# Identity products of other widths, the first chunk's gates loaded first, and another order in front of the first block

## The chip, the cores and the metric

The kernel runs on one core of a Trainium2 chip. The metric is device time in microseconds of one execution. A smaller time is better. Engines are called by the profile's names: PE (TensorE matmul), PEld (its weight loads), DVE (VectorE), ACT (ScalarE), POOL (GpSimd), SP (SyncE, whose queue issues nearly all DMAs).

## What is computed

A gated linear attention with 4 batches of 8 heads, 768 tokens and head size 40, followed by a two-layer network over the 3072 tokens with softplus between its layers:

```python
for t in range(S):
    m_new = np.maximum(f_gate[:, :, t] + m, i_gate[:, :, t])
    f_stab = np.exp(f_gate[:, :, t] + m - m_new)
    i_stab = np.exp(i_gate[:, :, t] - m_new)
    C = f_stab * C + i_stab * np.einsum('bhd,bhe->bhde', vt, kt)
    n = f_stab * n + i_stab * kt
    y[:, :, t] = sigmoid(o_gate[:, :, t]) * np.einsum('bhde,bhe->bhd', C, qt) / np.maximum(np.abs(nq), 1.0)
x = y.transpose(0, 2, 1, 3).reshape(B * S, H * D)      # 3072 x 320
h = x @ w_in                                           # 320 x 2048
g = np.maximum(h, 0.0) + np.log1p(np.exp(-np.abs(h)))
out = g @ w_out                                        # 2048 x 320
```

The weights arrive as 64-bit floats and are taken apart on the chip.

## The kernel before

The recurrence is done in chunks of 128 tokens (six per batch). A step is one chunk of one batch; 24 steps in the order of `ORDER`, which begins with the first chunk of each batch (steps 0 to 3 are named 1_0, 2_0, 0_0 and 3_0 in tile names). Three steps make a token tile of 384 rows, and 16 blocks of the hidden layer are computed for each of the eight tiles. A block is eight products into one PSUM bank `hp` (`X` against the high and low parts of `w_in`, `wih` and `wil`, L1154 for the first 32 blocks and L1006 later), softplus on ACT (L908, L910), the low part on DVE (`gl`, L916), and nine products into three banks `po` (L988, later L1006). The first block needs the whole of `X0`, that is, all of steps 0 to 2.

In front of the first block stand, in this order of need:

- **The gates.** `first_gates` (L167) loads the gates of the first chunk (`g0`, L172), scans them on DVE, takes the exponent on ACT, and spreads the result over partitions with small products by an identity matrix: `spread` (L163, into bank `po1`, copied out as `gT`) and, in `decays`, L429 (into `hp`, scanned by DVE at L445 as `pw`). `later_gates` (L216) does the same for the other chunks in two parts, tiles `gt0` and `gt1`, whose input gates are spread by `spread_inputs` (L206, copied to `gT` at L214). L156 spreads the decays of `gt0` into the pair of banks `pa`.
- **Steps 0 to 2.** Each has scores (L499), states (L516), a copy `cp`, values (L615 and L623) into a pair of banks (`pa` or `po2`), their sum on DVE (`y1z` L462, `yy` L644), a gate on POOL (`x`, L669), three transposes on PE (L752) and two halves of `X` on ACT and DVE.
- **The weights** of the first blocks, taken apart by `single` (L277 on), each part on the engine that `PICK` names (V DVE, G POOL, A ACT).
- **Identity products.** `keep_warm` (L771) multiplies the identity matrix by itself, `k` units of 128 columns, up to `cols` units in one product, into `po1`; nobody reads the result. Such a product of 32-bit floats shows as two records in the trace. Where it stands is called `k0`, `k1` and so on in `WHEN`; its `k` stands in `WARM`, its `cols` in `COLS`.

The program is recorded in the order of the numbers in `WHEN`, from low to high (a negative number is before the first block, a positive one counts products from there), and `in_order` (L114) makes each engine run its instructions in the recorded order. So the table decides what stands behind what on each engine, on SP's queue too. DMAs are all issued by SP but three. Behind the first blocks the same table runs the other steps among the products.

Of the kernel before, what the change touches and what calls it, by code (L numbers as in the profile page):

```python
# [18 lines left out]
L = 128  # L19
# [12 lines left out]
NCHAIN = B * H  # L32
# [12 lines left out]
def mlstm_moe_kernel(  # L45
# [121 lines left out]
    def first_gates():  # L167

        nc.vector.memset(fg0, 0.0)
        fg, ig = g0[:NCHAIN, 0], g0[:NCHAIN, 1]  # L170
        m = p1.tile([NCHAIN, L + 1], F32, tag="y1", name="m0")
        nc.sync.dma_start(g0[:NCHAIN], gates[:, :, 0:L].rearrange("g p s -> p g s"))  # L172
# [598 lines left out]
    def keep_warm(k, cols):  # L771
        assert not begun
        for i in range(0, k, cols):
            n = min(cols, k - i)
            nc.tensor.matmul(wm[:, 0:n], ident, ident.unsqueeze(1).broadcast_to([128, n, L]), start=True, stop=True)  # L775
# [431 lines left out]
    def finished(t):  # L1207
        return all(s in ended for s in range(t * NG, (t + 1) * NG))

    WHEN = {'l0': -292.75, 'p0': -281.3125, 'p1': -293.5, 'l1': -277.507812, 'p2': -277.578125, 'wl0': -278,  # L1210
# [186 lines left out]
```

## Time and profile before

| | us |
|---|---|
| three runs | 426.43, 429.14, 429.2 (median 429.14) |
| the profiled execution, whole time | 427.4 |
| its span, first to last instruction | 425.6 |
| PE busy | 418.3 (98%) |
| DVE busy | 272.8 (64%) |
| ACT busy | 210.8 (50%) |
| POOL busy | 62.8 (15%) |

The profiled execution lies inside the range of the three runs; 1.8 us of its time lie around the span. PE's share of busy time counts the identity products too, and the page's chain that ended last is PE for 93% of the span.

### The profile page before, as it was taken

The numbers are of one execution on the slowest core, as the hardware profiler recorded it, in microseconds if no ns is written. First come the engines' busy times: TensorE is split into PE (matmuls) and PEld (weight loads), VectorE is DVE, ScalarE is ACT, GpSimd is POOL, SyncE is SP. The second block draws the span as 40 slices with busy tenths as digits, with TensorE's granted clock in tenths as the row PEclk, the third lists the DMA queues.
The fourth block names the chain that finished last, engine by engine and source line by source line (L and its number), as shares of the span: only waits on it lengthen the run. The fifth ranks groups of instructions, "written<-read, shape, count | busy, mean of one in ns | idle before, by whom it ended". The sixth has DMA issues, their size and how long they took to land.

```text
span 425.6 us, 16026 instructions
## 1 busy us (share of the span) xinstructions
PE 418.3 (98%) x6866; PEld 403.9 (95%) x6866; DVE 272.8 (64%) x544; ACT 210.8 (50%) x443; POOL 62.8 (15%) x104
## 2 busy tenths in 40 slices
PE   8899999999999999999999999999999999999996
PEld 7789989999999999999999999999999999999996
DVE  6788899496867776749566675758567664522221
ACT  5588996776536243634336443534335433333332
POOL 2544634244454000000000000000000000000000
PEclk9999999999999999999999999999999999999999
DMA  6895975755275746173364536284264330001001
GB/s 192 269 294 165 271 217 156 223 176 162 64 193 160 189 118 185 49 204 93 76 171 116 127 115 163 64 159 138 67 186 104 74 114 24 2 2 48 2 3 48
DMA packets 51240, 55.17 MB, mean 130 GB/s; under 512 B 5568, under 2 KB 41312, under 8 KB 51168
## 3 DMA queue, kind: packets, MB, share of 16 engines
q1 hardware_dynamic: 50736, 53.65, 45.9%
q8 instruction: 54, 0.88, 0.8%
q10 hardware_dynamic: 432, 0.49, 0.4%
q14 instruction: 18, 0.15, 0.2%
HBM read 45.97 MB, written 8.14 MB: 127 GB/s over the span
## 4 chain that ended last, share of the span: by engine, by line
PE 93%; ACT 2%; DMA 1%; issue 1%; SPq 1%; DVE 1%; POOL 1%; ACTq 0%; POOLq 0%
PE hp L1006 31%; PE po L1006 29%; PE po L988 9%; PE hp L1154 8%; PE po L775 3%; PE hp L499 3%; PE pa L683 2%; PE pa L695 2%; DMA flast<-fl_d 1%; PE hp L516 1%; PE hp L429 1%; PE pa L499 1%; PE pa L516 0%; PE po L163 0%; PE pa L623 0%
## 5 line engine op out<-in xcount | busy, mean ns | idle before, releaser
L1006 PE MATMUL hp<-X,wih 64*128 64x384 f32 x1056 | 177.6, 337 | 0.0
L908 ACT ACTIVATE gh<-hp 128x384 fp32r<-128x384 f32 x80 | 39.3, 491 | 176.3 <-PE hp L1006 150.6
L1006 PEld LDWEIGHTS hp<-X,wih 64*128 64x128 f32 x1056 | 123.8, 185 | 1.8 <-POOLq L1017 0.3
L1006 PE MATMUL po<-woh,g 64*128 64x320 f32 x564 | 123.4, 306 | 0.1
L916 DVE TENSOR_TENSOR gl<-full,gh 128x384 fp32r<-128x384 f32 x48 | 26.8, 558 | 94.3 <-ACT full L910 93.8
L1006 PE MATMUL hp<-X,wil 64*128 64x384 f32 x384 | 81.2, 333 | 0.0
L1006 PEld LDWEIGHTS po<-woh,g 64*128 64x128 f32 x564 | 78.5, 185 | 0.0
L1006 PE MATMUL po<-woh,gh 64*128 64x320 f32 x294 | 68.0, 310 | 0.0
L1006 PE MATMUL po<-wol,gh 64*128 64x320 f32 x294 | 66.7, 306 | 0.0
L1006 PE MATMUL po<-woh,gl 64*128 64x320 f32 x294 | 66.4, 305 | 0.0
L1006 PE MATMUL po<-wol,g 64*128 64x320 f32 x282 | 63.9, 306 | 0.0
L1006 PEld LDWEIGHTS hp<-X,wil 64*128 64x128 f32 x384 | 58.0, 185 | 0.0
L910 ACT ACTIVATE full<-hp 128x384 f32<-128x384 f32 x96 | 46.7, 487 | 0.0
L1154 PE MATMUL hp<-X,wih 128*128 128x384 f32 x192 | 45.1, 341 | 0.3 <-DVE gl L916 0.3
L1006 PEld LDWEIGHTS po<-woh,gh 64*128 64x128 f32 x294 | 42.3, 184 | 0.0
L1006 PEld LDWEIGHTS po<-woh,gl 64*128 64x128 f32 x294 | 41.3, 185 | 0.0
L1006 PEld LDWEIGHTS po<-wol,gh 64*128 64x128 f32 x294 | 41.2, 185 | 0.0
L1006 PEld LDWEIGHTS po<-wol,g 64*128 64x128 f32 x282 | 39.2, 184 | 0.3 <-issue 0.3
L1154 PEld LDWEIGHTS hp<-X,wih 128*128 128x128 f32 x192 | 33.1, 188 | 1.0 <-DVE gl L916 0.6
L916 DVE TENSOR_TENSOR g<-full,g 128x384 fp32r<-128x384 f32 x48 | 26.7, 557 | 10.6 <-PE po L1006 7.2
L445 DVE TENSOR_TENSOR_SCAN pw<-fb,ident 128x512 f32<-128x512 f32 x21 | 26.6, 1268 | 0.0
L908 ACT ACTIVATE g<-hp 128x384 fp32r<-128x384 f32 x48 | 23.7, 493 | 0.1
(185 smaller groups left out, 700.0 us busy)
## 6 DMA issues: line engine op xcount, KB each, us to landing
vt<-in_vk SPq DMA_DIRECT2D x24, 324.0 KB
qk<-in_qk SPq DMA_DIRECT2D x48, 160.0 KB
fb<-fz_d SPq DMA_DIRECT2D x42, 128.0 KB
wo<-in_w_out SPq DMA_DIRECT2D x8, 640.0 KB
wr<-in_w_in SPq DMA_DIRECT2D x8, 512.0 KB
eg<-in_oT SPq DMA_DIRECT2D x6, 576.0 KB
yd<-y SPq DMA_DIRECT2D x36, 96.0 KB
out<-ob SPq DMA_DIRECT2D x21, 160.0 KB
```

The lines of the kernel that those rows point to most:

```text
L429: nc.tensor.matmul(z.fb[y * Q : (y + 1) * Q, j, :], ident[:, k : k + 1].broadcast_to([128, Q]), fg0, start=True, stop=True,)
L445: nc.vector.tensor_tensor_scan(z.pw.rearrange(flat), z.fb.rearrange(flat), ident4.rearrange(flat), 0.0, ALU.mult, ALU.add)
L499: nc.tensor.matmul(z.ga[x][y * Q : (y + 1) * Q, (i * NQ + q) * Q : (i * NQ + q + 1) * Q], z.k[rows, g, ts], z.q[rows, g, ts], start=True, ...
L683: nc.tensor.matmul(gc[out, x, c0 : c0 + Q], (z.cm if q else z.old)[rows, g * E : g * E + w], z.q[rows, g, q * Q : (q + 1) * Q], start=True ...
L695: nc.tensor.matmul(gc[i * PP : i * PP + w, y, c0 : c0 + Q], z.via[rows, e0 : e0 + w], z.pm[rows, j, q * Q : (q + 1) * Q], start=True, stop ...
L775: nc.tensor.matmul(wm[:, 0:n], ident, ident.unsqueeze(1).broadcast_to([128, n, L]), start=True, stop=True)
L908: nc.scalar.activation(gh, hp, AF.Softplus)
L910: nc.scalar.activation(full, hp, AF.Softplus)
L916: nc.vector.tensor_tensor(gl, full, gh, op=ALU.subtract)
L988: nc.tensor.matmul(po[j], a[:, j * 128 : (j + 1) * 128], w[:, f, :], start=(first and left[j] == 2), stop=(last and left[j] == 0),)
L1006: nc.tensor.matmul(out, *a, **k)
L1154: nc.tensor.matmul(hp, a, r, start=(i == 0), stop=(i == len(seq) - 1))
```

## The change

Three edits of code. The DMA of `g0` is issued ahead of the memsets that it waited for, so the zeroing of `g0` leaves out the partitions that it writes and becomes two memsets. `keep_warm` can put small products (32 rows out, 16 columns, line 775 of the kernel after) ahead of its units, as many as a new table `SMALL` says. And the tables change: nearly all numbers of `WHEN`, `COLS` (up to three units in one product), `WARM`, and some of `PICK`. All lines behind L172 move down by one to eight.

```diff
     def first_gates():
 
-        nc.vector.memset(fg0, 0.0)
+        nc.sync.dma_start(g0[:NCHAIN], gates[:, :, 0:L].rearrange("g p s -> p g s"))
+        nc.vector.memset(fg0[NCHAIN:64], 0.0)
+        nc.vector.memset(fg0[64:128], 0.0)
         fg, ig = g0[:NCHAIN, 0], g0[:NCHAIN, 1]
         m = p1.tile([NCHAIN, L + 1], F32, tag="y1", name="m0")
-        nc.sync.dma_start(g0[:NCHAIN], gates[:, :, 0:L].rearrange("g p s -> p g s"))
...
-    def keep_warm(k, cols):
+    def keep_warm(k, cols, small):
         assert not begun
+        for _ in range(small):
+            nc.tensor.matmul(wm[0:32, 0, 0:16], ident[:, 0:32], ident[:, 0:16], start=True, stop=True)
...
-    COLS = {0: 2, 2: 2, 3: 1, 4: 1, 6: 1, 7: 1, 9: 1, 10: 1, 11: 1, 12: 1, 17: 2, 20: 1}
-    WARM = {0: 15, 1: 2, 2: 1, 3: 3, 4: 2, 5: 3, 6: 3, 7: 4, 8: 0, 9: 2, 10: 3, 11: 4, 12: 2, 13: 0, 14: 2, 15: 4,
-        16: 1, 17: 2, 18: 1, 19: 0, 20: 4, 21: 0}
+    SMALL = {8: 0, 17: 0, 2: 0, 0: 0, 14: 0, 3: 0, 9: 0, 19: 0, 13: 4, 4: 0, 7: 0, 18: 0, 15: 0, 1: 0, 6: 2, 5: 0,
+        10: 0, 20: 0, 16: 1, 21: 0, 11: 0, 12: 0}
+    COLS = {0: 2, 2: 1, 3: 1, 4: 3, 6: 1, 7: 3, 9: 2, 10: 2, 11: 1, 12: 1, 17: 1, 20: 1, 5: 1, 15: 3, 18: 2, 14: 2,
+        19: 3, 21: 1, 8: 3, 1: 3, 13: 3, 16: 3}
+    WARM = {0: 15, 1: 1, 2: 4, 3: 4, 4: 1, 5: 4, 6: 0, 7: 0, 8: 0, 9: 1, 10: 5, 11: 2, 12: 4, 13: 0, 14: 2, 15: 7,
+        16: 0, 17: 0, 18: 4, 19: 0, 20: 0, 21: 0}
...
-            once(f"k{k}", us(at), keep_warm, WARM.get(k, n), COLS.get(k, 2))
+            once(f"k{k}", us(at), keep_warm, WARM.get(k, n), COLS.get(k, 2), SMALL.get(k, 0))
```

On PE, between the scores of the second step (into `po2`) and the states that follow, stood before (`hp`, `pa`, `po` are PSUM banks, `gt` the later gates, `ident` the identity matrix):

```order
L775 MATMUL po_80<-ident 128x128 x3
L775 MATMUL po_80<-ident 128x256
L615 MATMUL pa<-cp_0_263,qk_0_191 64x41 x8
L623 MATMUL pa<-vi_0_261,pw_0_232 64x41 x16
L163 MATMUL po_80<-ident,gt_128 64x16 x8
L775 MATMUL po_80<-ident 128x256 x2
L775 MATMUL po_80<-ident 128x128 x2
```

At the same place on PE stands now:

```order
L778 MATMUL po_80<-ident 128x128 x4
L163 MATMUL po_80<-ident,gt_160 64x16 x8
L616 MATMUL pa<-cp_0_285,qk_0_191 64x41 x8
L624 MATMUL pa<-vi_0_303,pw_0_223 64x41 x16
L778 MATMUL po_80<-ident 128x128 x5
```

The spread of `gt0` has gone from behind the values of the first step (L615, L623) to ahead of them, so that it no longer stands right in front of identity products, which write the bank that ACT copies `gT` from.

On PE, at the first two blocks and a half, stood before (the third transposes of `X0` first; `hp_72`, `hp_73`, `hp_74` are the banks of blocks 0, 1 and 2):

```order
L775 MATMUL po_80<-ident 128x128 x4
L752 MATMUL hp_74<-ident,x_0_589 128x128 x3
L775 MATMUL po_80<-ident 128x128 x4
L1154 MATMUL hp_72<-X_564,wih 128x384 x2
L775 MATMUL po_80<-ident 128x128 x3
L1154 MATMUL hp_72<-X_564,wih 128x384 x2
L1154 MATMUL hp_72<-X_564,wil 128x384 x2
L1154 MATMUL hp_72<-X_564,wih 128x384 x2
L1154 MATMUL hp_73<-X_564,wih 128x384 x2
L156 MATMUL pa<-ident,d_342 128x32 x2
L1154 MATMUL hp_73<-X_564,wih 128x384 x2
L615 MATMUL pa<-cp_0_654,qk_0_434 64x41 x8
```

At the same place on PE stands now:

```order
L775 MATMUL po_80<-ident 32x16 x6
L778 MATMUL po_80<-ident 128x128 x2
L753 MATMUL hp_74<-ident,x_0_614 128x128 x3
L778 MATMUL po_80<-ident 128x256 x2
L778 MATMUL po_80<-ident 128x128
L775 MATMUL po_80<-ident 32x16
L1157 MATMUL hp_72<-X_584,wih 128x384 x4
L1157 MATMUL hp_72<-X_584,wil 128x384 x2
L1157 MATMUL hp_72<-X_584,wih 128x384 x2
L1157 MATMUL hp_73<-X_584,wih 128x384 x4
L616 MATMUL pa<-cp_0_649,qk_0_434 64x41 x8
L624 MATMUL pa<-values_in,pw_0_512 64x41 x16
```

The three units inside the first block are gone, and L156 has left block 1: it comes five products behind the values of the fourth step (L624), in front of the second product of block 2, and both write `pa`.

On SP's queue the program began with these DMAs (`g` the first chunk's gates, `gt` the later ones, `wr` the first weights):

```order
L223 DMA gt_128<-in_gates 32x2x256
L172 DMA g_103<-in_gates 32x2x128
L223 DMA gt_142<-in_gates 32x2x384
L317 DMA wr_152<-in_w_in 128x2x512
L320 DMA wr_152<-in_w_in 64x256 x2
```

It begins with these now:

```order
L169 DMA g_103<-in_gates 32x2x128
L224 DMA gt_136<-in_gates 32x2x384
L224 DMA gt_160<-in_gates 32x2x256
L318 DMA wr_166<-in_w_in 128x2x512
L321 DMA wr_166<-in_w_in 64x256 x2
```

The first chunk's gates have moved up one place, and the 256 columns of `gt0` went from first to third.

## Rows read from the trace of the kernel before

**Rows 1.** The page, part 1: busy time, share of the span, instructions.

```profile
PE 418.3 (98%) x6866; PEld 403.9 (95%) x6866; DVE 272.8 (64%) x544; ACT 210.8 (50%) x443; POOL 62.8 (15%) x104
```

**Rows 2.** Busy time by stretch: engines' us (instructions), granted clock, DMA share, GB/s.

```profile
16.48:32.87 16.39, 16.04 (x369) 14.39 (x369) 12.99 (x29) 13.76 (x23) 7.19 (x10) 1.00 0.87 271
32.87:100.00 67.13, 66.57 (x844) 62.18 (x843) 55.17 (x104) 53.48 (x113) 30.58 (x43) 1.00 0.70 201
100.00:422.00 322.00, 321.88 (x5435) 315.79 (x5433) 192.40 (x384) 135.68 (x296) 17.72 (x28) 1.00 0.39 102
```

**Rows 3.** The chain that ended last, first 70 us: start, us, what (x records).

```profile
1.71 5.31 PE po L775 x16
...
10.21 0.85 PE po L775 x4
...
13.17 1.30 PE po L775 x8
...
15.41 1.07 issue
...
16.81 0.59 PE po L163 x16
...
17.42 0.22 ACT gT L214
...
17.69 1.57 PE po L775 x8
...
21.73 1.28 PE po L775 x6
...
23.63 1.09 PE po L775 x8
...
25.32 1.31 PE po L775 x10
...
30.45 1.09 PE po L775 x8
```

**Rows 4.** Timeline of PE: start, us, line, tiles, shape, records, idle before.

```profile
17.69 1.57 PE L775 MATMUL po<-ident 128*128 128x256 f32 x8 [0.31 <-ACT gT L214]
...
31.97 1.06 PE L775 MATMUL po<-ident 128*128 128x128 f32 x8
32.87 0.60 PE L1154 MATMUL hp<-X,wih 128*128 128x384 f32 x2
33.31 0.83 PE L775 MATMUL po<-ident 128*128 128x128 f32 x6
34.02 0.62 PE L1154 MATMUL hp<-X,wih 128*128 128x384 f32 x2
...
34.82 0.86 PE L1154 MATMUL hp<-X,wih 128*128 128x384 f32 x4
35.60 0.63 PE L156 MATMUL pa<-ident,d 32*128 32x32 f32 x4
```

**Rows 5.** Timeline of DVE, same columns.

```profile
3.21 0.47 DVE L178 TENSOR_TENSOR_SCAN m<-g,m 32x128 f32<-32x128 f32 x1 [2.05 <-DMA g<-in_gates]
...
8.43 1.22 DVE L445 TENSOR_TENSOR_SCAN pw<-hp,ident 128x512 f32<-128x512 f32 x1 [0.29 <-PE hp L429]
...
32.17 0.56 DVE L796 CAST X<-hp 128x384 fp32r<-128x384 f32 x1 [0.21 <-PE hp L752]
...
37.96 0.50 DVE L462 TENSOR_TENSOR y1z<-pa,fcT 64x328 f32<-64x328 f32 x1 [1.14 <-PE pa L623]
38.50 0.50 DVE L644 TENSOR_TENSOR yy<-pa,y1z 128x328 f32<-128x328 f32 x1
```

**Rows 6.** Timeline of SP's queue: the issue of the first chunk's gates.

```profile
1.19 0.41 SPq L172 DMA_DIRECT2D g<-in_gates  x1
```

**Rows 7.** DMA queues from 13 to 17 us: packets, MB, share of 16 engines.

```profile
q1 hardware_dynamic: 556, 1.26, 96.4%
q8 instruction: 1, 0.02, 2.1%
```

More of the change, by code (lines that the diff above doesn't have):

```diff
@@ L1208, in finished @@
         return all(s in ended for s in range(t * NG, (t + 1) * NG))
-    WHEN = {'l0': -292.75, 'p0': -281.3125, 'p1': -293.5, 'l1': -277.507812, 'p2': -277.578125, 'wl0': -278,
[65 rows of a table removed]
-    COLS = {0: 2, 2: 2, 3: 1, 4: 1, 6: 1, 7: 1, 9: 1, 10: 1, 11: 1, 12: 1, 17: 2, 20: 1}
-    WARM = {0: 15, 1: 2, 2: 1, 3: 3, 4: 2, 5: 3, 6: 3, 7: 4, 8: 0, 9: 2, 10: 3, 11: 4, 12: 2, 13: 0, 14: 2, 15: 4,
-        16: 1, 17: 2, 18: 1, 19: 0, 20: 4, 21: 0}
+    WHEN = {'l0': -278.414062, 'p0': -302.25, 'p1': -300.25, 'l1': -303.25, 'p2': -279.449219, 'wl0': -278,
[66 rows of a table added]
+    SMALL = {8: 0, 17: 0, 2: 0, 0: 0, 14: 0, 3: 0, 9: 0, 19: 0, 13: 4, 4: 0, 7: 0, 18: 0, 15: 0, 1: 0, 6: 2, 5: 0,
[4 more added lines that the diff above has]
+        16: 0, 17: 0, 18: 4, 19: 0, 20: 0, 21: 0}
     PICK = {'wl2': 'V', 'oh6': 'G', 'wl3': 'V', 'mgi7': 'V', 'ol1': 'V', 'ol3': 'V', 'wh5': 'A', 'wi61': 'V',
         'ol2': 'V', 'mgo5': 'V', 'wi50': 'V', 'ol5': 'V', 'gb0': 'V', 'wi01': 'A', 'wl1': 'V', 'xh2': 'V',
[1 row of a table removed]
[1 row of a table added]
         'mgi5': 'A', 'wi51': 'G', 'wm50': 'G', 'wh6': 'V', 'wl6': 'V', 'cq8': 'V', 'gc1': 'V', 'vi2': 'V',
[2 rows of a table removed]
[2 rows of a table added]
         'wl4': 'V', 'x5': 'V', 'vi6': 'A', 'cq6': 'V', 'mgi6': 'V', 'old7': 'A', 'cp7': 'V', 'cq7': 'V', 'wi60': 'G',
```

148 rows, old and new, of tables (PICK, WHEN) are left out of this document.

## The prediction

> **What bounds the kernel now.** The page's busy times come first [rows 1]: PE is busy for 98% of the span and the next engine, DVE, for 64%. A mean over stages doesn't say what a change in one stage is worth, so the second view is busy time by stretch [rows 2]. From 32.87 us, where the first block's first product starts [rows 4], to 100 us PE is busy for 66.57 of 67.13 us, and from 100 to 422 us for 321.88 of 322.00. From the first block on the time is PE's own work, and an order that frees another engine there has 0.6 us to win at most. The third view, the chain that ended last [rows 3], shows what a busy PE in front of the block is worth: a good part of it is L775, the identity products, whose result nobody reads. So the time can move in two ways: by the moment at which the first block begins, and by PE time behind it that is no product of a block.
>
> **Identity products.** Each is two records. Counted in units of 128 columns there were 15 at the start (5.31 us), then groups of 3, 5, 6, 5, 4, 5, 4, 4 and 4, and 3 more inside the first block, 58 in all. The order has 54 now: the same 15, then 4, 4, 5, 2, 7, 5, 1, 4, 2 and 5, none in the block, and seven small ones. The chain has most of the old groups [rows 3]: 0.85, 1.30, 1.57, 1.28, 1.09, 1.31 and 1.09 us, sum 8.49. The group at 31.97 us lasts until 32.87, 0.90, with transposes and wide products as neighbours, and a group of four that has transposes ahead of it is put at the same; the one in the block lasts from 33.31 to 34.02, 0.71 [rows 4]. Together 11.00 us behind the first 15.
>
> The new groups are priced from these. Four single units take 1.09 and five take 1.31 [rows 3]: 0.22 a unit, and 1.09 - 0.88 = 0.21 for coming from smaller products and going back. About half of that, 0.1, is left where one neighbour is 128 wide, as the 0.90 shows. A double takes (1.28 - 0.21 - 0.22) / 2 = 0.43. No triple is in the trace: between three halves of a double, 0.65, and three singles, 0.66; I take 0.65. No small one is either: the nearest row is the eight spreads of L163, 0.59 us, 0.07 each, and the lower bound is nothing; I take 0.07, as their shape is nearly the same. Then the groups are 4: 1.09; 4: 1.09; 5: 1.31; a double: 0.64; two triples and a single: 1.30 + 0.22 + 0.21 = 1.73; two doubles and a single: 1.28; a single: 0.32; 4 beside transposes: 0.98; six small and two singles: 0.42 + 0.44 + 0.10 = 0.96; two doubles, a single and a small one: 0.86 + 0.22 + 0.12 = 1.20. Sum 10.60, of which all stands in front of the block. **Term: 10.60 - 11.00 = -0.40**, made of +0.31 in front and -0.71 in the block; between -0.9 (small ones free) and 0.
>
> **The first chunk's gates first: 0.** The first scan waited 2.05 us for this DMA, which was issued at 1.19 us behind `gt0` [rows 5, 6]; without that DMA's issue, of its own length, ahead of it, it can land about 0.4 us sooner. But what the gates feed on PE, the spreads at L163 and L429, stand behind the 15 identity units, which still end at 1.71 + 5.31 = 7.02 us, and DVE's first `pw` scan at 8.43 waits for those spreads, not for gates [rows 5]. The cover is PE's own filling; without it the gain would be 0.4. The later `gt0` lands behind one DMA more, and its scan stands behind the first chunk's in any case. One decoding step of the first weights has moved from ACT to DVE, ahead of that `pw` scan. It isn't in the trace in this form; below it costs nothing (0.29 us of idle time in front of the scan), above as much as the scan itself, 1.22 us [rows 5], less this idle time. Behind it wait `pw`, POOL's `vw` and the first states on PE, and in front of these PE now has a group of four identity units, 1.09 us, and the spread for the third step, which has moved up; so 0.
>
> **The spread of `gt0` moved ahead.** Before, identity products at 17.69 waited 0.31 us until ACT had copied `gT` out of their bank (copy 17.42, 0.22 us) [rows 3, 4]. Now the spread stands ahead of the first step's values, which cover the copy. **Term: -0.31**; 0 if another copy is late at the next identity group (the part 1 spread has a 256-column unit and the second step's values behind it first).
>
> **The wait at 15.41.** In the middle of L623's equal products PE stood for 1.07 us, and the chain calls it "issue": nothing that the profile shows was waited for [rows 3]. In 13 to 17 us the program's DMAs took 96.4% of the DMA engines, and one packet of an instruction queue was among them [rows 7]. I read it as PE having run out of fetched instructions. If the fetch ends at a given moment, the 0.59 us of L163's spread [rows 3], which now runs before the wait and not behind it, fills that much of it: -0.59. If the fetch is set off by PE's own progress, the wait moves along and keeps its length: 0. **Term: -0.30**, half way; the bounds are -1.07 (gone) and +1.07 (once more elsewhere). [...]
>
> **L156 behind the values.** This spread writes `pa`. Before, it came ahead of the values of the fourth step. Now it comes five products behind them, and DVE has to read those values out of `pa` first: 37.96 to 39.00, 1.04 us for `y1z` and `yy` [rows 5]. Five products cover (35.60 - 34.82) / 4 = 0.20 each [rows 4] at most, so some 0.9 to 1.0, and a wait of 0.1 is left with DVE free at once. DVE had 1.14 us idle before `y1z`, but the values now come about 0.6 us sooner in PE's order, since L156 (0.63 us at 35.60) has left its place ahead of them. **Term: +0.25**, between 0 and 0.8. Behind L156 in PE's queue wait the rest of block 2 and all blocks.
>
> The other moves in the tables (weights on other engines, later steps, DMAs of `wr2` ahead of `fz_d`) lie beside the full PE of [rows 2] and are put at 0, within the 0.56 us that PE stood idle from 32.87 to 100.
>
> **Sum: -0.40 - 0.31 - 0.30 + 0.25 = -0.76.** The first block's first product comes 0.3 us sooner (about 32.6), and what follows gains 0.71 and loses 0.25. On the profiled execution's 427.4 us that gives 426.6. The median of the three runs is 429.14, which would give 428.4; the four executions known lie from 426.43 to 429.2, so a median of the changed kernel can fall anywhere between, and I put it at 427.3.
>
> **The rivals.**
> - *Nothing moves* (chance 0.25). The identity products were filling in waits, and what is taken out comes back as idle time in front of X0: the last cast of X0 ended at 32.73 [rows 5], 0.14 us ahead of the first block. For it speaks that short distance; against it that groups of 4 to 6 units stood ahead of work whose inputs were long there, and that the 0.71 in the block had ready products on both sides. It gives 427.4 by the profiled execution, 428.1 by the same reckoning as above.
> - *Slower: L156 takes the place of the waits removed* (0.12). If DVE reaches `y1z` more than a microsecond late, PE stands before block 2 for that long. It decides once the wait is over 0.25 + 0.76 = 1.0 us. DVE has weights and `gl` of block 0 ahead of it, each 0.5 to 1.2 us. With 2 us the sum is +1.0: 428.4 by the profiled execution, 429.1 as above.
> - *The clock falls* (0.05). [...] Less filling can mean more idle time. The price is in the start: the first 15 units took 5.31 us, and seven doubles and a single at later prices are 3.3, so one stay at the low level cost 2.0 us. It gives 428.6 to 429.3. [...]
> - *Both waits go* (0.08): the 1.07 at 15.41 vanishes and the small products cost nothing: -0.9 - 0.31 - 1.07 + 0.1 = -2.2, 425.2 by the profiled execution, 425.9 as above.
>
> **How the numbers follow.** The forecast has 0.50. The terms' bounds add up to -2.3 and +1.9 on 427.4, 425.1 to 429.3; with the spread of the runs at both ends I take 424.8 to 429.8. One per cent, 4.3 us, is about what a measurement of this kernel can tell from no change, and no case reaches it. What is left for it is the spread of the runs, 2.8 us, on top of the outer cases: faster 0.05, same 0.91, slower 0.04.
>
> **What would show it.** In the profile after: the first block's first product near 32.6; PE standing less than 1.07 us inside the first step's values and not at all before the identity units that follow; no identity product after the first block begins; a wait of 0 to 0.8 us before L156; PE full from 100 us on. Wrong would be a first block at 33 us or later, a wait of over 1 us before block 2's second product, a granted clock under 1.00, or PE idle for over 1 us between 33 and 100 us.

## The result, and the profile after

The changed kernel takes 429.97 us against 428.23 us, medians of 22 runs each; the ratio is 1.0054, 95% interval 1.0036 to 1.0071 (the quotient of these medians is 1.0041). Three of the changed kernel's runs (435 to 438 us, granted clock 0.98) and the profiled run of block_new below (434.44 us, 0.98) were in a slower state, and the ratios leave such runs out. The change is about half a per cent slower, and the forecast was 0.2% faster. The profiled execution takes 428.87 us, 1.47 more than that of before, with a span of 427.1 us.

The page of the kernel after, part 1, answers to [rows 1]:

```profile
PE 419.0 (98%) x6866; PEld 404.3 (95%) x6866; DVE 274.2 (64%) x549; ACT 211.4 (49%) x444; POOL 62.3 (15%) x99
```

The page says nothing of the loss: PE is busy for the same 98%. Busy time by stretch does [rows 2], here of the kernel after:

```profile
16.48:32.87 16.39, 15.75 (x355) 13.25 (x350) 13.42 (x30) 12.91 (x21) 7.77 (x10) 1.00 0.95 281
32.87:100.00 67.13, 65.09 (x834) 60.75 (x833) 55.55 (x106) 53.30 (x115) 29.37 (x39) 1.00 0.66 195
100.00:422.00 322.00, 321.72 (x5433) 316.14 (x5432) 192.66 (x384) 137.06 (x296) 17.98 (x28) 1.00 0.40 104
```

PE's idle time from 32.87 to 100 us has gone from 0.56 to 2.04 us. So the loss lies behind the start of the first block, where the prediction had written 0. Two rows of PE hold most of it (timeline of PE after: start, us, line, tiles, shape, records, idle before and what ended it); the three rows above them are from the front:

```profile
21.09 0.44 PE L624 MATMUL po<-vi,pw 64*64 64x41 f32 x16 [0.18 <-issue]
...
31.63 0.55 PE L753 MATMUL hp<-ident,x 128*128 128x128 f32 x3 [0.46 <-POOL x L670]
...
33.36 1.32 PE L1157 MATMUL hp<-X,wih 128*128 128x384 f32 x4
...
53.27 0.44 PE L1157 MATMUL hp<-X,wil 128*128 128x384 f32 x1 [0.84 <-DVE wil L340]
54.18 0.68 PE L616 MATMUL pa<-c,qk 40*64 40x41 f32 x32 [0.47 <-DVE X L763]
```

DVE is named, but the timeline of DVE after shows that it had stood idle itself shortly before, for `gl`, and that `wil` and `X` were queued behind that:

```profile
27.11 1.26 DVE L302 SCALAR_TENSOR_TENSOR sgo<-mago,sgo 128x640 uint32<-128x640 uint32 x1
28.41 0.50 DVE L463 TENSOR_TENSOR y1z<-po,fcT 64x328 f32<-64x328 f32 x1
...
32.69 0.67 DVE L248 TENSOR_TENSOR_SCAN d<-gt,d 32x256 f32<-32x256 f32 x1
...
33.47 0.54 DVE L763 TENSOR_TENSOR X<-hp,X 128x384 fp32r<-128x384 f32 x1
...
50.19 0.56 DVE L919 TENSOR_TENSOR gl<-hp,gh 128x384 fp32r<-128x384 f32 x1 [2.10 <-ACT hp L913]
...
52.26 0.95 DVE L340 TENSOR_TENSOR wil<-sgi,wih 128x512 fp32r<-128x512 f32 x1
...
53.56 0.56 DVE L763 TENSOR_TENSOR X<-pa,X 128x384 fp32r<-128x384 f32 x1
```

And ACT after, which `gl` waited for:

```profile
46.71 0.43 ACT L799 COPY cp<-pa 104x328 f32<-104x328 f32 x1 [1.25 <-POOL c L595]
47.04 0.80 ACT L288 ACTIVATE mago<-wo 128x640 f32<-128x640 f32 x1
47.73 0.95 ACT L294 ACTIVATE sgo<-wo 128x640 uint16<-128x640 uint32 x1
48.53 0.92 ACT L298 ACTIVATE sgo<-wo 128x640 f16<-128x640 f32 x1
49.30 0.48 ACT L911 ACTIVATE gh<-hp 128x384 fp32r<-128x384 f32 x1
49.66 0.50 ACT L913 ACTIVATE hp<-hp 128x384 f32<-128x384 f32 x1
```

The table has put the fifth step's copy `cp` on ACT (it was on DVE), where it waits 1.25 us, and 2.67 us of decoding of the second `w_out` pair right behind it, ahead of block 4's softplus (L911, L913). The softplus is late, `gl` with it, and DVE, which runs its instructions in the recorded order, holds back `wil` and `X` for PE.

In before neither ACT's softplus of that block, nor DVE's copy and `gl`, nor PE's product with `c`, the one that waits 0.47 us above, waited (timelines of ACT, DVE and PE before):

```profile
47.73 0.47 ACT L908 ACTIVATE gh<-hp 128x384 fp32r<-128x384 f32 x1
```

```profile
48.11 0.49 DVE L796 COPY cp<-pa 104x328 f32<-104x328 f32 x1
48.61 0.56 DVE L916 TENSOR_TENSOR gl<-hp,gh 128x384 fp32r<-128x384 f32 x1
```

```profile
51.61 0.68 PE L615 MATMUL pa<-c,qk 40*64 40x41 f32 x32
```

Last, far from all this, PE's waits from 75 us on, of the kernel after (sum, times, longest):

```profile
PE hp L1157 <- DVE gl L919: 0.3, 1, 0.3
PE po L1009 <- issue: 0.3, 1, 0.3
```

The first stood in before as well. The second is one more of PE's waits called issue: 0.26 us, until 152.07.

To place a loss, the table below compares each trace with that of before: the records of the blocks' products (3712 in each) are counted through, and the start of the k-th is compared with the k-th of before. Each trace is of one execution. "3rd" is the moment of the first block's third product, the first one that reads the low part of `X0` (the texts quoted below call it the second). "Loss 51-54" is how far the 91st record has fallen back against the 82nd; "behind" is the last record against the 82nd. "Fetch front" and "fetch 150" are PE's waits called issue from 5 to 33 us, and at about 150 us. "First 15" is the length of the first 15 identity units.

| kernel | first 15 | fetch front | 3rd | loss 51-54 | fetch 150 | behind | ratio to before (95%) |
|---|---|---|---|---|---|---|---|
| before | 5.31 | 1.1 | 34.02 | - | 0 | - | - |
| control | 6.46 | 0 | 33.88 | -0.06 | 0 | -0.24 | 0.9969 (0.9935 to 1.0002) |
| no_inblock | 5.36 | 1.1 | 37.52 | -0.01 | 0 | -0.58 | 1.0028 (0.9997 to 1.0059) |
| scan_behind | 6.08 | 0 | 33.29 | 0.00 | 0 | -0.50 | 0.9996 (0.9952 to 1.0040) |
| gates_first | 5.89 | 1.1 | 34.61 | 0.00 | 0.2 | +0.27 | 1.0014 (0.9971 to 1.0058) |
| cp4_only | 6.53 | 1.5 | 35.64 | -0.02 | 0 | 0.00 | 1.0035 (0.9997 to 1.0073) |
| cp4_w21 | 5.04 | 0.7 | 33.59 | 1.30 | 0 | +0.41 | 1.0060 (1.0030 to 1.0090) |
| front_new | 5.70 | 0 | 33.54 | 0.18 | 0 | +0.13 | 1.0043 (1.0014 to 1.0071) |
| sgo_front_new | 5.41 | 0 | 33.40 | 0.13 | 0 | +0.03 | 0.9981 (0.9955 to 1.0008) |
| short_front | 6.41 | 0 | 33.25 | -0.11 | 0 | -0.21 | 1.0007 (0.9970 to 1.0044) |
| after | 5.92 | 0.2 | 34.06 | 1.34 | 0.3 | +1.57 | 1.0054 (1.0036 to 1.0071) |
| after_again | 5.96 | 1.2 | 35.11 | 1.35 | 1.1 | +2.34 | 1.0025 (0.9990 to 1.0060) |
| sgo_behind | 5.11 | 1.1 | 33.92 | 1.34 | 1.1 | +2.92 | 1.0005 (0.9975 to 1.0035) |
| cp4_back | 5.80 | 1.0 | 34.36 | 0.34 | 0.5 | +0.99 | 1.0043 (1.0018 to 1.0068) |
| w21_back | - | 0.6 | 34.56 | -0.11 | 1.4 | +1.45 | 1.0057 (1.0033 to 1.0081) |
| block_new | 4.96 | 1.2 | 38.37 | 1.77 | 0.8 | +2.83 | 1.0046 (1.0015 to 1.0076) |
| weights_old | 4.96 | 1.3 | 34.36 | 1.34 | 0.7 | +4.21 | not timed |
| steps_old | 5.05 | 0.8 | 33.82 | -0.30 | 0.6 | +0.55 | not timed |

(w21_back's chain of waits goes by another way in its first microseconds, so it has no such row.)

### The profile page after: what moved, and what is told of

It reads as the page before. It is cut to its first block, busy times and chain, and to the rows that moved or that the text cites. A ratio compares the mean times of both kernels' runs of the same rounds, so it can differ in the third digit from the quotient of the medians.

```text
span 427.1 us, 16028 instructions
## 1 busy us (share of the span) xinstructions
PE 419.0 (98%) x6866; PEld 404.3 (95%) x6866; DVE 274.2 (64%) x549; ACT 211.4 (49%) x444; POOL 62.3 (15%) x99
## 4 chain that ended last, share of the span: by engine, by line
PE 92%; DVE 4%; ACT 2%; issue 1%; POOL 0%; ACTq 0%; DVEq 0%; POOLq 0%
PE hp L1009 31%; PE po L1009 29%; PE hp L1157 9%; PE po L991 9%; PE hp L500 3%; PE po L778 2%; PE pa L684 2%; PE pa L696 2%; PE hp L517 1%; PE hp L430 1%; PE pa L616 1%; PE pa L624 0%; DVE sgo L302 0%; ACT gh L911 0%; PE po L163 0%
## 5 line engine op out<-in xcount | busy, mean ns | idle before, releaser
L911 ACT ACTIVATE gh<-hp 128x384 fp32r<-128x384 f32 x80 | 39.2, 490 | 175.1 <-PE hp L1009 150.3
L1009 PEld LDWEIGHTS hp<-X,wih 64*128 64x128 f32 x1056 | 122.5, 185 | 1.5 <-issue 0.2
L1009 PE MATMUL po<-woh,g 64*128 64x320 f32 x564 | 121.8, 305 | 0.0
L1009 PEld LDWEIGHTS po<-woh,g 64*128 64x128 f32 x564 | 76.2, 184 | 0.0
L1009 PE MATMUL po<-woh,gh 64*128 64x320 f32 x294 | 66.9, 310 | 0.0
L1009 PE MATMUL po<-wol,gh 64*128 64x320 f32 x294 | 65.4, 306 | 0.0
L1009 PE MATMUL po<-wol,g 64*128 64x320 f32 x282 | 62.8, 307 | 0.3 <-issue 0.3
L913 ACT ACTIVATE full<-hp 128x384 f32<-128x384 f32 x96 | 46.7, 487 | 0.0
L1009 PEld LDWEIGHTS po<-woh,gh 64*128 64x128 f32 x294 | 41.3, 185 | 0.0
L1009 PEld LDWEIGHTS po<-woh,gl 64*128 64x128 f32 x294 | 40.0, 184 | 0.0
L1009 PEld LDWEIGHTS po<-wol,gh 64*128 64x128 f32 x294 | 40.0, 184 | 0.0
L919 DVE TENSOR_TENSOR gl<-hp,gh 128x384 fp32r<-128x384 f32 x32 | 17.4, 550 | 12.1 <-ACT hp L913 12.0
```

Source lines behind the costliest of these rows:

```text
L911: nc.scalar.activation(gh, hp, AF.Softplus)
L913: nc.scalar.activation(full, hp, AF.Softplus)
L919: nc.vector.tensor_tensor(gl, full, gh, op=ALU.subtract)
L1009: nc.tensor.matmul(out, *a, **k)
```

## The experiments

Theory A: the loss is made behind the first block. Theory B: it is made in front of it. The kernels mix the two tables; a name is that of a place in `WHEN` or `PICK`.

**Which half loses: front_new and block_new.** The first has the front of the change and the old places and engines behind the first block, the second the reverse.

> The changed kernel with its new identity products, gate loading and order in front of the first block, but with the places and engines of everything behind the first block (steps from the fourth on, weights from the third pair on, gt0's and gt1's later parts) as before. Theory A (the loss is made behind the block, where wil and X come late at 53 to 54 us): the waits before the products at 53.3 (0.8 us) and before the values at 54.2 (0.5 us) are gone, and the time is 1.3 us below the changed kernel's 430.0, about 428.7; by the in-block units (-0.7) it should be no slower than before's 428.2 by more than 0.5. Theory B (the loss is made in front of the block, by X0's late third step and the wait before L156): it stays at 430.0, 1.8 above before, and block products past 100 us come 1.0 us or more later than before. Chance of the first 15 identity units' clock rise (theory C): their group lasts 5.3 or 5.9 us in any kernel, whatever its order.

> The kernel before with its own front, but with the changed kernel's places and engines for everything behind the first block. Theory A (loss behind the block): waits of 0.5 to 0.9 us before products at about 53 us and time 1.3 us above before, about 429.5. Theory B (loss in front): within 0.4 us of before, 428.2.

Behind the 82nd record front_new loses 0.13 us, block_new 2.83 (0.9 of it between the 91st and the 301st record, where the granted clock was at half for 3.4 us), with the loss at 51 to 54 in full. Its late first block (38.37) is the clock too, which was at half for 10.2 us from 18.3 us on. Theory A holds in the traces. These two times don't show it: the ratios are 1.0043 and 1.0046.

**What a ratio is worth: control and after_again.** An empty line added to each of the two kernels.

> The kernel before with an empty line added, so the same instructions. If a kernel that is launched beside the one before takes the same time, the ratio is 1.000 within 0.002, and the 1.0043 of the changed kernel with the old block part, whose trace is 0.6 us shorter than that of before, is a loss that the one trace doesn't show. If the 1.003 to 1.0046 of the four kernels so far comes from the comparison itself, this one too shows 1.003 or more, about 1.5 us.

> The changed kernel with an empty line added, on the same chip as the others of this call: 1.0054 times before (1.0036 to 1.0071), about 428.4 where before takes 426.1. Its trace shows a second time what is fixed in its front (X0's third transposes waiting about 0.5 us for POOL's gate; 0.5 and 0.8 us waits at 53 to 54 us) and what is not (the end of the first 15 identity units, 5.3 to 5.9 us long; waits called issue, 0 to 1.1 us in sum).

The same instructions take 0.3% less in control, just within the error and outside both numbers expected. So a ratio of 1.004 to one side is no proof of a change of 1 us, and the steps below are judged by their traces. Front_new's 1.0043 stays unexplained: its trace is of the fastest of its twelve runs. After_again against control is 429.1 to 427.08 us, +0.5%; against before itself, timed beside both, it is 1.0025, and that interval holds 1.

Taken together the ratios lean to theory A. Their mean is 1.0009 for eight kernels with the old block part (without cp4_w21, which has the two moves shown below) and 1.0038 for the six with the new one, 1.2 us apart, though the two groups overlap. Sgo_front_new and sgo_behind, timed together, differ in the block part alone: medians 427.14 and 428.39 us. That is 1.25 us, but before and control, the same instructions, lay 1.40 apart there.

**The loss at 51 to 54 us.** cp4_back: the changed kernel, with

```diff
-    'cp4': 46.662851          PICK 'cp4': 'A'
+    'cp4': 59.4375            PICK 'cp4': 'V'
```

> The changed kernel with one thing put back: the copy of the fifth step's states, cp4, on VectorE and at its old place, 13 products later. If theory A's chain is right (the copy waits 1.25 us on ScalarE at 46.7 us, the softplus of that block waits behind it, gl waits 2.10 us on VectorE, and wil and X behind gl come late), the 2.10 us wait of gl is gone, the waits at 53.3 and 54.2 fall from 1.3 us to under 0.5, and the time is 0.8 to 1.3 us below 430.0: 428.7 to 429.2. If the lateness comes from other moved weights (the third w_in tensor's two parts, now on VectorE, and w_out's second one, moved 10 products), gl's wait goes but wil stays late: 429.8 to 430.0. Theory B: 430.0.

Of 1.34 us 0.34 are left, as expected; the ratio, 1.0043, shows nothing of it. The reverse, cp4_only, is before with that one move made:

> The kernel before with one thing taken from the changed one: the copy of the fifth step's states, cp4, on ScalarE and 13 products sooner. If that copy alone makes the loss at 53 us, ScalarE's softplus queues behind it, gl waits about 2 us on VectorE and the products between 51 and 54 us come 1.0 to 1.3 us later against before: 1 us or 0.25% slower. If it takes the other moved weights too, the loss is under 0.4 us.

No loss at all. The copy alone is not enough: on ACT the softplus still comes right behind it (timeline of ACT, cp4_only):

```profile
49.46 0.41 ACT L796 COPY cp<-pa 104x328 f32<-104x328 f32 x1
49.77 0.48 ACT L908 ACTIVATE gh<-hp 128x384 fp32r<-128x384 f32 x1
...
50.98 0.94 ACT L297 ACTIVATE sgo<-wo 128x640 f16<-128x640 f32 x1
```

So the second `w_out` pair's decoding was added, and taken away from the changed kernel:

```diff
 cp4_w21 (before, cp4 as in the change, and)
-    'w2_1_0': 38.578187, 'w2_1_1': 42.37525, 'w2_1_2': 65.9165, 'w2_1_5': 69.945578
+    'w2_1_0': 48.62764, 'w2_1_1': 53.5, 'w2_1_2': 47.645246, 'w2_1_5': 88.523321
 w21_back (after, and the reverse)
```

> The kernel before with two things of the changed one: the copy cp4 on ScalarE at its new place, and the decoding steps of the second w_out pair (mago, sgo, sgo) at theirs, right behind that copy and ahead of block 4's softplus (before and with the copy alone, the softplus stands ahead of the last one). Theory: the softplus is late behind the copy's wait and 2.7 us of decoding, gl holds up VectorE by about 2 us, and TensorE loses 1.0 to 1.3 us between 51 and 54 us of its program, as in the changed kernel (1.34). Rival: the loss needs the weights that moved to VectorE (wi21, wm31) too: under 0.5 us here, as with the copy alone (0.35).

> The changed kernel with only the decoding steps of the second w_out pair put back to before's places; the copy cp4 stays on ScalarE at its new place. By the same theory the softplus of block 4 comes directly behind the copy, and the loss at 51 to 54 us falls from 1.34 to under 0.5 us. Rival: the copy itself, waiting 1.25 us for its input, is enough: 0.8 or more stays. The late instruction fetch at about 152 us (0.2 to 1.1 us in all five traces with the new block part, none in those with the old) is expected to stay, if it comes of the order behind 55 us, and to go, if it comes of the loss at 53 us, which moves TensorE against the DMAs.

1.30 us with both, -0.11 without the second. ACT, PE and DVE of cp4_w21:

```profile
46.45 0.43 ACT L796 COPY cp<-pa 104x328 f32<-104x328 f32 x1 [1.14 <-POOL c L594]
46.78 0.80 ACT L287 ACTIVATE mago<-wo 128x640 f32<-128x640 f32 x1
...
49.04 0.47 ACT L908 ACTIVATE gh<-hp 128x384 fp32r<-128x384 f32 x1
```

```profile
52.49 0.68 PE L615 MATMUL pa<-c,qk 40*64 40x41 f32 x32 [1.53 <-DVE X L762]
```

```profile
49.92 0.56 DVE L916 TENSOR_TENSOR gl<-hp,gh 128x384 fp32r<-128x384 f32 x1 [2.32 <-ACT hp L910]
```

and DVE of w21_back, where `gl` no longer waits:

```profile
48.28 0.67 DVE L530 TENSOR_TENSOR pw<-pa,pw 128x512 f32<-128x512 f32 x1
48.88 0.54 DVE L919 TENSOR_TENSOR gl<-hp,gh 128x384 fp32r<-128x384 f32 x1
```

The wait at 51 to 54 us is shown from both sides in the traces: it takes the two moves together. The copy by itself costs nothing (cp4_only), the decoding with the copy put back 0.34 us (cp4_back). That a kernel is faster without this wait is not shown: the ratios of cp4_back and w21_back, 1.0043 and 1.0057, are no lower than those of the kernels that have it. In the trace of w21_back the wait called issue at 152 us is the longest one there of all traces (PE's waits from 75 us on):

```profile
PE po L1009 <- issue: 1.4, 1, 1.4
```

**The fetch at 150 us.** In all six traces so far with the whole or nearly the whole new block part PE waits there, for 0.3 to 1.4 us; in the ten with the old one for 0, once for 0.2. W21_back has lost the wait at 53 and keeps this one (1.4), so the one doesn't hang on the other. Two halves were put back:

> The changed kernel with the places and engines of all weight decoding and weight loading behind the first block as before; steps and gates stay new. The late instruction fetch at about 150 us: if it comes from the weights' part, its wait on TensorE (0.3 to 1.4 us in all six traces with the new block part, 0 to 0.2 in the ten with the old) is at most 0.2 here; if it comes from the steps' and gates' part, it is 0.3 us or more. The loss at 53 us stays under 0.5 us, as with the second w_out pair alone put back.

> The other half: the changed kernel with the steps and gates behind the first block as before, cp4 on VectorE too, and the second w_out pair's decoding at before's places; the other weights stay new. If the late instruction fetch comes from the weights' part, its wait at about 150 us is 0.3 us or more; if it comes from the steps' and gates' part, at most 0.2. If both halves show it or neither does, it hangs on no single half, and its cause stays open.

Both still wait, 0.7 and 0.6 us: it hangs on no single half, and its cause is open. Weights_old missed its other number, under 0.5: it loses 1.34 us at 51 to 54, by a road of its own (`wil` stood behind `wol`, and PE waited 1.38 us for it), after which the granted clock fell to 0.50 for 3.4 us.

**The front.** No_inblock is before with `WARM[10]` 0 for 3, so without the three units in the first block.

> The kernel before without the three identity units inside the first block, nothing else changed. The prediction's term: the block's products follow each other at once and all that comes later is 0.7 us sooner, 427.5 against 428.2. Rival (the units filled a wait, the weights' low part or block 1's inputs come no sooner): 0.0 to -0.2, with idle time of 0.5 us on TensorE between 33 and 38 us.

The rival's way: the ninth record comes no sooner against the first (0.01 us later), and PE waits instead. PE and DVE of no_inblock:

```profile
36.37 0.59 PE L1154 MATMUL hp<-X,wih 128*128 128x384 f32 x2
37.52 0.63 PE L1154 MATMUL hp<-X,wih 128*128 128x384 f32 x2 [0.55 <-DVE X L762]
```

```profile
36.14 0.67 DVE L247 TENSOR_TENSOR_SCAN d<-gt,d 32x256 f32<-32x256 f32 x1
36.85 0.16 DVE L248 COPY fl_s<-d 32x4 f32<-32x4 f32 x1
36.92 0.54 DVE L762 TENSOR_TENSOR X<-hp,X 128x384 fp32r<-128x384 f32 x1
```

The units covered X0's last low part, and that stood behind the scan of `gt0`'s decays. Scan_behind removes the units and also records that scan (`l8`: -187.58, now -100) behind the low part.

> The kernel before without the three identity units in the first block, and with VectorE's scan of gt0's decays (0.67 us and a copy of 0.16) moved from ahead of X0's last low part to behind it. Theory X (the units only covered the wait for that low part, which ended at 33.96 us, and the scan ahead of it made the wait): with the units away and the scan behind, the low part ends 0.7 to 0.8 us sooner and the wait of 0.55 us that the removal alone showed is gone; from the first to the ninth record the block is 0.6 to 0.7 us shorter than before's, and the ninth comes that much sooner counted from X0's last cast. Rival (TensorE's products were the limit, the 0.55 us was chance): the same 0.02 us as with the removal alone. L156 waits for that scan and may give back up to 0.3. Whole time: 427.5 to 428, of which one launch can hide all.

Now the ninth record comes 0.65 us sooner against the first, and the first products run on (PE of scan_behind):

```profile
32.79 1.12 PE L1154 MATMUL hp<-X,wih 128*128 128x384 f32 x4
```

Of that 0.47 is given back by 49.5 us, at transposes that wait for `wih`. In the changed kernel one more instruction stands in X0's chain: `sgo` (1.26 us at 27.11), ahead of the third step's `y1z`. Sgo_behind records it behind `yy` (`w0_1_3`: -201.45), as before had it; sgo_front_new does the same on front_new.

> The changed kernel with one VectorE instruction moved: the decoding of the first w_out pair (sgo, 1.26 us at 27.11) goes from ahead of the third step's y1z to behind its yy, where before had it. Theory B (front): y1z starts when its values are there, 0.7 us sooner, X0 too, TensorE's 0.46 us wait in front of X0's third transposes is gone and the blocks come 0.4 to 0.5 us sooner: time 0.4 us below the changed kernel's. Theory A: the waits at 53 to 54 us are unchanged, so the gain comes back only as far as the wait in front of the transposes; between 0 and -0.4.

> The changed front with that same instruction moved, and the places and engines behind the first block as before. Both theories together: the 0.46 us wait in front of X0's third transposes gone and no waits at 53 to 54 us, so 0.4 us less than the kernel with the new front alone (1.0043) and 1.7 us less than the changed kernel: 426.8 to 427.4 where before takes 426.1. If its trace is shorter than that of before but its median longer, what differs from run to run (the clock's rise and falls, issue waits) decides and not the order.

In sgo_behind `y1z` starts at 27.65 and not at 28.41, when its values are there, and PE's wait for POOL's gate is 0.26 us and not 0.46; the third product comes at 33.92 and not at 34.06, with 0.9 us more of fetch and first units 0.8 shorter ahead of it. That is 0.14 and not the 0.4 to 0.5 expected; the scan still stood ahead of the low part. Sgo_front_new has the third product 0.14 sooner than front_new, too; its ratio, 0.9981 for 1.0043, fell by far more than that, and no trace shows why. Short_front puts all of it together on front_new: `sgo` behind the gate product (-200.9), the scan behind the low part (`l8` -20), two units (`WARM[10]`) instead of five before the first block.

> The changed front with the old block part, VectorE's decoding of the first w_out pair moved behind the third step's gate product, the scan of gt0's decays behind X0's last low part, and two identity units instead of five between X0's last transposes and the first block. If the third step's chain on VectorE sets the moment of the first block's second product (34.0 us in both kernels): that moment comes 1.0 to 1.4 us sooner than in the kernel with the new front alone, 32.1 to 32.7 us where the clock rises at 5.5 to 6.5 us, and the time is 1 us or more under before's. If TensorE's own work in front sets it: 0.3 to 0.7 sooner (the three units left out).

The third product comes at 33.25, 0.3 us sooner than in front_new, with first units that took 0.7 longer. That is less than the 1.0 hoped for, at the lower end of the rival's 0.3 to 0.7, and the time is that of before, 1.0007. Gates_first is before with the first edit alone.

> The kernel before with the first edit alone: the first chunk's gates are issued at the head of the queue, the zeroing is split in two. The prediction's term is 0: the first scan on VectorE comes about 0.4 us sooner, but TensorE's spreads of its results still start at 7.0 us behind 15 identity units (later where the clock rises later), and X0's first block within 0.2 us of before. Rival: the second load's shift makes a later wait of up to 0.5 us.

Its first scan starts at 3.03 us and not at 3.21, and the first block 0.60 us later than before's; the first 15 units were 0.58 longer. So the edit alone is worth 0. But it does not put `g` at the head of the queue, as the text above has it: with the old table `g` still goes second, at 1.19 us. The move to the head is in the changed table: in the kernel after, `g` is issued at 0.75 us (1.19 in [rows 6]), the scan starts at 2.54 (3.21 in [rows 5]), and the 15 units still end 5 us later, at 7.63. So that is worth 0 too, as forecast.

## Why the prediction was wrong, step by step

Between the two profiled executions the forecast was -0.76 us, and +1.47 was measured. Of these 2.2 us 1.05 are there by the ninth product (-1.01 forecast: -0.30 in front and -0.71 in the block; +0.04 measured), and 1.34 come at 51 to 54 us; all the rest together is -0.2.

- **The other moves at 0** is the step that failed, for the larger part. The prediction took the 0.56 us for which PE stood idle from 32.87 to 100 as what the moves there could win or lose. It bounds what a better order can win. It says nothing of what a worse one can lose, since a full PE is full only as long as nothing comes late. The sum lacked 1.3 us at 51 to 54 (in every trace with both moves) and the rest at 150 us and later, whose cause is open; from the 82nd record on the changed kernel falls back by 1.57, 2.34 and 2.92 us in three traces (after, after_again, sgo_behind). The two rows were there to be read: `cp4` from V to A in `PICK`, and ACT's order around it. No rival stood behind the first blocks but L156.
- **Identity products, -0.40**: wrong, and the other step that failed. The -0.71 in the block was no gain, since those units covered a wait: no_inblock gives nothing, and scan_behind gives 0.65 once the wait has been moved too. The rule that they had ready products on both sides was right for the first two products, and wrong for the third, which reads the low part of `X0` that ended at 33.96 (timeline of DVE before):

```profile
32.64 0.67 DVE L247 TENSOR_TENSOR_SCAN d<-gt,d 32x256 f32<-32x256 f32 x1
...
33.42 0.54 DVE L762 TENSOR_TENSOR X<-hp,X 128x384 fp32r<-128x384 f32 x1
```

The prices of the eight new groups without small products were right within 0.02 us each, from one start to the next; the two with them took 1.19 and 1.34 for 0.96 and 1.20. So in front the groups cost 0.58 us more than before's, and not 0.31.
- **In front**: the first product comes at 33.36 and not at 32.6, which the prediction had named as a sign of being wrong, as it had PE's idle time of over 1 us between 33 and 100 (2.04). DVE's chain (`sgo`, `y1z`, scan, `X`) set the third: 34.06 against 34.02. That looks like the first rival ("nothing moves"), as does the 82nd record, -0.09 us from that of before, but it is luck in part: in this execution the first 15 units took 0.6 longer and the fetch wait was 0.9 shorter. In after_again, with a fetch wait like before's (1.2 for 1.1), the third product comes 27.44 us behind the end of those units, and in before 27.00.
- **`gT`, -0.31**: the wait is gone, as forecast, but PE now waits 0.46 us for POOL's gate before X0's third transposes.
- **The wait at 15.41, -0.30**: the reading as instruction fetch fits the packets of the last section (each such wait ends 1.2 to 1.6 us behind the end of one), the term doesn't hold. The wait comes or goes from one execution to the next: 1.1 us in before's trace, 0 in control with the same instructions, and from 0 to 1.3 in the ten traces with the changed front.
- **L156, +0.25**: right. From the ninth to the 61st record, behind L156 and the values in both, the changed kernel falls back by 0.17 us, and front_new, with L156 at its old place, by 0.00.
- **The gates first, 0**: right (gates_first, and the end of the first 15 units in after).
- **The clock** was 1.00 in all three stretches after; in this pair of traces that rival was not the cause. That idle time brings the clock down was an assumption, and no run shows it: PE's idle time from 32.87 to 100 us went from 0.56 to 2.04 us, and the clock stayed at 1.00.

## What to carry to other kernels

A table of moves is to be read where the wait can be made, not where time is idle now: for each instruction that changes its engine or place, look at what it waits for and what stands behind it on its new engine, up to the next thing that the full engine needs. Filling that nobody reads gives its time back only if the product behind it has its inputs (no_inblock gave 0 of 0.71 us, scan_behind 0.65); look for the last of those inputs and what stands ahead of it. And with changes of 1 us in 430, a trace in which events are counted through tells more than a ratio: the same instructions, launched anew, came out 0.3% apart. But a trace is one execution: what it shows of a wait is to be looked for in a second one.

## What the runs showed of the hardware

PE's waits called issue go with packets of the instruction queue, and so the text calls them fetch. In before the packet of the instruction queue lies between 13.7 and 15.2 us, and PE waits 1.07 us; in control it lies between 12.2 and 13.6, and PE waits for nothing (DMA queues of before, 13.7 to 15.2 us: packets, MB, share of 16 engines):

```profile
q8 instruction: 1, 0.02, 5.6%
```

and of control, 12.2 to 13.6 us:

```profile
q8 instruction: 1, 0.02, 5.0%
```

All 18 traces fit this. In eight the packet starts between 11.6 and 12.3 us, and PE has no such wait before 20 us; in ten it starts between 13.6 and 15.4, and PE waits 0.6 to 1.5 us. Each of the 24 waits called issue in these traces, those at 150 us too, ends 1.2 to 1.6 us behind the end of a packet of that queue. So the wait goes with a late packet. That PE stands because the packet brings its instructions is a reading of these times; why the start differs between two executions of the same instructions is open.

Most packets of that queue come without such a wait: before has 54 of them and one wait, after 54 and two. Two places, at 15 and at 150 us, cost from 0 to 1.5 us (in three traces there are waits of 0.2 to 0.7 at 20 to 28 us as well), with the program's own DMAs taking 85 to 95% of the DMA engines around the first (before and control, 12.2 to 15.2 us).

The first 15 identity units, the same in each kernel, took from 4.96 to 6.53 us; the two longest are of kernels with before's own front (chain of control, against 5.31 in [rows 3]):

```profile
1.71 6.46 PE po L775 x16
```

The clock's rise comes at another moment in another execution: the record of the granted clock begins, as full, at 5.40 us in before, at 6.62 in after, at 7.71 in control, and from 4.68 (block_new) to 7.85 (cp4_only) in all. In before the records of the first 15 units start 0.43 us apart ahead of that moment (2.29 to 5.28 us) and 0.22 apart behind it (5.56 to 6.42). It also fell again in three traces: in weights_old (55.9 us, for 3.4), twice in block_new (18.3 us, for 10.2, and 59.3 us, for 3.4), and in no_inblock. In no_inblock, whose front is that of before word for word, it was at half (0.50) from 19.1 us on for 6.8 us (busy time by stretch of no_inblock), and the first block began 3.5 us later:

```profile
19.20:25.90 6.70, 6.70 (x113) 6.07 (x112) 2.71 (x8) 4.84 (x9) 1.77 (x3) 0.50 0.69 230
```

PE was busy for all of that stretch; ahead of it lay the fetch wait of 1.1 us and the 0.3 for `gT`, which in before's trace did not bring it down. In weights_old a wait of 1.38 us ended 1.8 us ahead of the fall, and in after waits of 0.84 and 0.47 us at 52 to 54 us brought none. What decides it is open.
